# Staging the expert weights of a routed feed-forward layer in eight quarters instead of four

## The chip, the cores and the metric

The kernel runs on one core of one Trainium2 chip. The metric is the device time of one execution in microseconds (us). The engines named below are TensorE (PE in the trace, its weight loads PEld), VectorE (DVE), ScalarE (ACT), GpSimd (POOL) and the queue of SyncE (SP), which issues most transfers.

## What is computed

Three layers follow each other. A recurrent attention gives 3072 tokens of 384 numbers. A dense feed-forward layer (384 to 2048 and back, with W_in and W_out) is applied to them. Then each token goes to the one of 8 experts with the largest gate value, and that expert's two matrices are applied:

```python
e_idx = np.argmax(logits, axis=1)
for e in range(E):
    mask = e_idx == e
    h = np.maximum(x[mask] @ w1[e], 0.0)          # 384 -> 1024
    out[mask] = gate_w[mask, None] * (h @ w2[e])  # 1024 -> 384
```

Results are single precision. Every operand of a large matmul is therefore kept as a sum of two half-precision parts, high and low, and each product is three matmuls: high by high, high by low, low by high.

## The kernel before

**The expert layer in blocks.** Tokens are sorted by expert into blocks of 256. The blocks 0, 1 and 2 (`NB` = 3) are chosen from the first 20 of 24 token tiles, while the dense layer still runs. The experts of the blocks from 3 on are known only when all tokens are routed: `final` writes them as the table `evi2`, and `final_b` the list of tokens in each block. In this run there are 14 blocks, 0 to 13; the last two hold at most 128 tokens each and stand behind branches (`rest`, L1162).

**One block.** `moe_gather` fetches the 256 rows (indirect DMA from POOL) into `G`, `moe_xm` transposes them by DMA into `XM` and copies the gate weights to `GC`. `moe_h(j, m)` computes one eighth (m = 0 to 7) of the hidden layer: nine matmuls into a PSUM bank (`psf` of two banks, or `psa` for m = 2 and 5), ACT's `mt` (ReLU, L881), ACT's `gg` (the high part, L882), and DVE's `gg` (the low part, L336, from `mt` and the high part). `mt` has two buffers: the third `mt` waits for the first's low part. `moe_o(j, t)` multiplies by the second matrix into `pso`, 24 matmuls for each half t of the tokens; the third matmul of every three needs the low part of `gg`. The result is scaled into `ob` and scattered to the output by POOL (L906).

**The weights of a block** come in four quarters q of 768 KB: two of the first matrix (q = 0, 1) and two of the second (q = 2, 3). `moe_w(j, q, e, 0)` loads a quarter into the staging area `SG[q]` from SP's queue (L851 and L853). `moe_w(j, q, None, 1)` converts it into high and low parts: two pieces, each one ACT instruction (L866) and one DVE instruction behind it (L867). The converted matrices are double buffered by parity of the block: W10 and W20 (in the trace `W`) hold even blocks, W11 and W21 odd ones. `SG[0]` and `SG[1]` are tiles of their own, `SG[2]` and `SG[3]` lie in the area `wi` of W_in, each part of which is free once the dense layer has read it for the last time. `conv_q(j, q)` converts quarter q of block j and then loads quarter q of block j + 1 into the same place.

**Block 1 in the program.** `moe_block(1)` runs when the second table appears (`fin`, L957): most of its `moe_o`, `final_b`, the rest of `moe_o`, the first hidden eighths of block 2, the gathers of blocks 3 and 4, and then `conv_q(2, q)` for all four q, which loads block 3.

**What sets the order.** The framework lists each engine's instructions at compile time by a planner that plays the program through with assumed costs. At run time each engine and each queue keeps that order and only waits for semaphores.

Of the kernel before, what the change touches and what calls it, by code (L numbers as in the profile page):

```python
# [10 lines left out]
F32 = mybir.dt.float32  # L11
# [21 lines left out]
MINB = NT // TB  # L33
MAXB = MINB + E - 1
NB = 3
# [18 lines left out]
SR, SA, SV, SS, SG, SX, SWI, SWO, SX2, SWG, SW1, SH2, SW2 = 8, 11, 12, 11, 14, 10, 5, 13, 13, 10, 13, 14, 13  # L54
# [75 lines left out]
def body(ctx, tc, r, k, v, w, u, rk, ul, w_in, w_out, mod, w_gate, bias, w1, w2, cst, out, dbg=None):  # L130
# [173 lines left out]
    z = 2 if wide else 1  # L304
# [521 lines left out]
    def moe_gather(j):  # L826
        idx = FT["idx"] if j < NB else FT["idx2"]
        g_ = G[j % 3]
        nr = NT if j >= NB else NF * 128
        for t in range(2):  # L830
            nc.gpsimd.indirect_dma_start(  # L831
                out=g_[:, t, :], out_offset=None, in_=scr[0:nr],
                in_offset=bass.IndirectOffsetOnAxis(ap=idx[:, 0, 2 * j + t:2 * j + t + 1], axis=0),
                bounds_check=nr - 1, oob_is_err=False,
            )
# [9 lines left out]
        return nc.sync.value_load(et, min_val=0, max_val=E - 1)  # L845

    def moe_w(j, q, e, part):
        st = SG[q]
        if part == 0:
            if q < 2:  # L850
                nc.sync.dma_start(st, w1[ds(e, 1), q].rearrange("e p x -> p (e x)"))  # L851
            else:
                nc.sync.dma_start(st, w2[ds(e, 1), q - 2].rearrange("e p x -> p (e x)"))  # L853
            return
        if q < 2:
            dst = W1[j % 2][:, :, :, 512 * q:512 * q + 512]
            sv, sc = st.rearrange("p (k f) -> p k f", k=KD), SW1
        else:
            dst = W2[j % 2][:, :, 4 * (q - 2):4 * (q - 2) + 4, :]
            sv, sc = st.rearrange("p (k f) -> p k f", k=4), SW2  # L860
        for z_ in range(2):
            if q < 2:
                o_, i_ = dst[:, :, :, 256 * z_:256 * z_ + 256], sv[:, :, 256 * z_:256 * z_ + 256]
            else:
                o_, i_ = dst[:, :, 2 * z_:2 * z_ + 2, :], sv[:, 2 * z_:2 * z_ + 2, :]
            nc.scalar.activation(o_[:, 0], i_, AF.Copy, scale=_pow2(sc))  # L866
            nc.vector.scalar_tensor_tensor(o_[:, 1], i_, _pow2(sc), o_[:, 0], op0=ALU.mult, op1=ALU.subtract)  # L867
# [50 lines left out]
    def load_q(j, q):  # L918
        if q == 0:
            RG[j] = moe_reg(j)  # L920
        moe_w(j, q, RG[j], 0)

    def conv_q(j, q, load=True):
        if CV.get(j, 0) > q:
            return
        CV[j] = q + 1
        with tc.issue_after(END["ib"]) if j in (NB - 1, NB) else ExitStack():
            moe_w(j, q, None, 1)
        if load:
            load_q(j + 1, q)  # L930

    def moe_block(j, nt=2, hook=None, done=0, ahead=0, conv=False, load=False, x=False):
        n = [0]

        def tick():
            if hook:
                hook(n[0])
            n[0] += 1

        def cv(q):  # L940
            if conv:
                conv_q(j + 1, q, load)

        fin = x and j == NB - 2
        if x and j + 2 <= MINB + 1 and j not in (NB - 2, NB - 1):
            moe_xm(j + 2)
        for m in range(NF2):
            tick()
            if m >= done:
                if m == max(done, 3) and not fin:  # L950
                    cv(0)
                moe_h(j, m, 128 * nt)
            if x and m == 5 and j >= NB - 1 and j + 3 <= MINB + 1:
                moe_gather(j + 3)
            if x and m == 5 and j == NB - 1:
                moe_xm(j + 2)
        if fin:  # L957
            for t in range(nt):
                tick()
                moe_o(j, t, 0, NF2 - 3)  # L960
            final_b()
            with tc.issue_after(PLM[0]):
                for t in range(nt):
                    moe_o(j, t, NF2 - 3, NF2)
                for m in range(ahead):
                    moe_h(j + 1, m)
            moe_gather(NB)
            moe_xm(NB)
            moe_gather(NB + 1)
            for q in range(4):  # L970
                cv(q)
            return
        for m in range(ahead):
            moe_h(j + 1, m)
        for t in range(nt):
            tick()
            cv(1 + t)
            moe_o(j, t, 0, NF2 - 3)
        if nt == 1:
            cv(2)  # L980
        cv(3)
        if x and j == MINB - 1:
            conv_q(j + 2, 0, False)
            conv_q(j + 2, 1, False)
        for t in range(nt):
            tick()
            moe_o(j, t, NF2 - 3, NF2)
# [93 lines left out]
    for n in range(NG * NU + LAG):  # L1081
# [11 lines left out]
        if mp is None and sp[0] == len(steps):  # L1093
# [3 lines left out]
            wif = wi.rearrange("p u a k f -> p (u a k f)")  # L1097
            SG = [mp.tile([128, 1536], F32, name=f"SG{i}") for i in range(2)]
            SG += [wif[:, 3072 * i:3072 * i + 3072].bitcast(F32) for i in range(2)]
            XM = [mp.tile([128, 2 * KD, TB], F16, name=f"XM{i}") for i in range(2)]  # L1100
            XM += [wif[:, 6144:6144 + 2 * KD * TB].rearrange("p (k t) -> p k t", t=TB)]
            G = [mp.tile([128, 2, XR], F32, name=f"G{i}") for i in range(2)]
# [143 lines left out]
```

## Time and profile before

| | us |
|---|---|
| median of 3 runs (lowest, highest) | 744.01 (743.41, 747.09) |
| the profiled execution | 748.82 |
| its span, first to last instruction | 747.1 |
| around the span (748.82 - 747.1) | 1.7 |
| PE busy in the span | 707.1 |
| DVE busy, ACT busy | 507.6, 490.5 |

The dense layer ends near 521 us; from 491 us on expert weights are converted, and from 552 us on blocks 2 to 13 run. The profile is of one execution, and a time in the span is counted from its first instruction.

### The profile page before, as it was taken

How to read it: one execution, taken by the hardware profiler on the slowest of the kernel's cores; microseconds unless marked ns; L12 is line 12 of the kernel's file. 1: busy time of each engine (PE TensorE's matmuls, PEld its weight loads, DVE VectorE, ACT ScalarE, POOL GpSimd, SP SyncE). 2: the span in 40 equal slices, each digit the busy share in tenths (PEclk: the TensorE clock that was granted, in tenths of full speed). 3: DMA queues.
4: the chain of work that ended last, by engine and by line, in shares of the span. 5: the costliest groups of instructions: out<-in, count | busy, mean ns of one | idle time of the engine just before them, and what ended most of it. 6: DMA issues, size and time to landing. Idle time of an engine off the chain costs nothing. (4 is left out here: it accounts for less than half of the span.)

```text
span 747.1 us, 17657 instructions
## 1 busy us (share of the span) xinstructions
PE 707.1 (95%) x6769; PEld 536.1 (72%) x6769; DVE 507.6 (68%) x1077; ACT 490.5 (66%) x955; POOL 425.1 (57%) x414
## 2 busy tenths in 40 slices
PE   4899989999999999999999999998998999999984
PEld 4768867777777777777777777776776777767763
DVE  5999984575746665667566645777785789666761
ACT  3568755667666677766666765477755977657752
POOL 5878888778677778877767660012053566231221
PEclk9999989999999999999999999999999999999998
DMA  9875343444423442354331202189439999899930
GB/s 296 264 229 189 125 112 81 122 102 112 101 76 91 118 105 58 100 124 102 80 79 55 32 13 33 54 254 303 142 90 329 374 343 333 244 246 238 258 122 13
DMA packets 89059, 114.77 MB, mean 154 GB/s; under 512 B 60709, under 2 KB 67018, under 8 KB 88964
## 3 DMA queue, kind: packets, MB, share of 16 engines
q1 hardware_dynamic: 84512, 102.75, 49.3%
q0 software_dynamic: 3456, 10.24, 4.3%
q8 instruction: 57, 0.93, 0.5%
q10 hardware_dynamic: 996, 0.53, 0.3%
q14 instruction: 38, 0.31, 0.2%
HBM read 90.29 MB, written 9.84 MB: 134 GB/s over the span
## 5 line engine op out<-in xcount | busy, mean ns | idle before, releaser
L538 PE MATMUL psf<-xT,wi 128*128 128x256 f16 x1728 | 212.9, 277 | 6.5 <-DVE e L547 4.6
L562 PE MATMUL pso<-wo,ring 128*128 128x384 f16 x1152 | 211.3, 327 | 0.8 <-ACT wo L301 0.4
L538 PEld LDWEIGHTS <-wi 128*128 128x128 f16 x1728 | 167.1, 99 | 35.3 <-issue 6.4
L562 PEld LDWEIGHTS <-ring 128*128 128x128 f16 x1152 | 110.7, 98 | 63.2 <-issue 2.0
L336 POOL TENSOR_TENSOR ring<-e,ring 128x512 f16<-128x512 f32 x80 | 92.5, 1157 | 55.0 <-ACT ring L549 51.9
L547 DVE SCALAR_TENSOR_TENSOR e<-e,psf 128x512 f32<-128x512 f32 x96 | 65.7, 685 | 83.0 <-ACT e L546 79.3
L895 PE MATMUL pso<-W,gg 128*128 128x384 f16 x624 | 111.0, 326 | 2.3 <-DVE gg L336 2.3
L875 PEld LDWEIGHTS <-W 128*128 128x128 f16 x1008 | 93.6, 99 | 22.8 <-issue 4.2
L549 ACT ACTIVATE ring<-e 128x512 f16<-128x512 f32 x96 | 60.1, 626 | 52.5 <-DVE e L547 52.2
L895 PEld LDWEIGHTS <-gg 128*128 128x128 f16 x624 | 60.1, 98 | 38.6 <-DVE gg L336 4.7
L906 POOL DMA_INDIRECT out_dram<-ob,idxb x20 | 36.2, 1808 | 86.3 <-DVE ob L905 45.4
L545 ACT ACTIVATE e<-psf 128x512 f32<-128x512 f32 x96 | 56.6, 590 | 31.9 <-PE psf L538 27.8
L546 ACT ACTIVATE e<-e,nel 128x512 f32<-128x512 f32 x96 | 69.1, 720 | 2.4
L867 DVE SCALAR_TENSOR_TENSOR W<-SG,W 128x768 f16<-128x768 f32 x56 | 52.3, 956 | 25.6 <-ACT W L866 25.3
L875 PE MATMUL psf<-XM,W 128*128 128x256 f16 (+1 forms) x540 | 61.3, 266 | 0.9 <-ACT mt L881 0.9
L866 ACT ACTIVATE W<-SG 128x768 f16<-128x768 f32 x56 | 45.3, 835 | 21.8 <-DMA SG<-in_w_dram 21.5
L867 DVE SCALAR_TENSOR_TENSOR W<-wi,W 128x768 f16<-128x768 f32 x56 | 52.0, 955 | 8.6 <-ACT W L866 7.4
L336 DVE TENSOR_TENSOR gg<-mt,gg 128x256 f16<-128x256 f32 (+1 forms) x112 | 43.5, 404 | 10.3 <-ACT gg L882 8.8
L866 ACT ACTIVATE W<-wi 128x768 f16<-128x768 f32 x56 | 44.8, 835 | 5.0 <-DMA wi<-in_w_dram 2.0
L882 ACT ACTIVATE gg<-mt 128x256 f16<-128x256 f32 (+1 forms) x112 | 42.6, 400 | 1.7
L350 DVE TENSOR_TENSOR_SCAN RK<-lw,bnd 112x520 f32<-112x520 f32 x24 | 34.5, 1439 | 8.0 <-ACT lw L349 4.6
L881 ACT ACTIVATE mt<-psf 128x256 f32<-128x256 f32 (+1 forms) x84 | 29.1, 360 | 15.8 <-PE psf L875 8.3
(268 smaller groups left out, 1142.4 us busy)
## 6 DMA issues: line engine op xcount, KB each, us to landing
SG<-in_w_dram SPq DMA_DIRECT2D x28, 768.0 KB, 7.0
wi<-in_w_dram SPq DMA_DIRECT2D x28, 768.0 KB, 5.5
stg<-in_w_in_dram SPq DMA_DIRECT2D x8, 768.0 KB, 4.9
stg<-in_w_out_dram SPq DMA_DIRECT2D x8, 768.0 KB, 4.3
ld<-in_rk_dram SPq DMA_DIRECT2D x16, 384.0 KB, 3.2
lw<-in_w_dram SPq DMA_DIRECT2D x24, 227.5 KB, 2.9
lr<-in_r_dram SPq DMA_DIRECT2D x24, 224.0 KB, 3.0
lk<-in_k_dram SPq DMA_DIRECT2D x24, 224.0 KB, 3.0
```

What stands on the lines that cost most here:

```text
L336: (nc.gpsimd if pool else nc.vector).tensor_tensor(lo, f, hi, op=ALU.subtract)
L538: mm = nc.tensor.matmul(ph[:, 256 * z_:256 * z_ + 256], lhsT=wi[:, u_, a, kk, 128 * z_:128 * z_ + 128], rhs=xg[:, b_ * KD + kk, :], start= ...
L545: nc.scalar.activation(e, ph, AF.Exp, scale=_pow2(-PH))
L546: nc.scalar.activation(e, e, AF.Identity, scale=_pow2(PH), bias=nel)
L547: LASTV[0] = nc.vector.scalar_tensor_tensor(e, e, 0.0, ph, op0=ALU.min, op1=ALU.max).ins
L549: LASTA[0] = nc.scalar.activation(hl[:, 0], e, AF.Copy).ins
L562: nc.tensor.matmul(po_[g][i][:, 0:DM], lhsT=hl[:, a, z_, 128 * i:128 * i + 128], rhs=wo[:, u_, b_, z_, :], start=(u_ + z_ + n == 0), stop= ...
L866: nc.scalar.activation(o_[:, 0], i_, AF.Copy, scale=_pow2(sc))
L867: nc.vector.scalar_tensor_tensor(o_[:, 1], i_, _pow2(sc), o_[:, 0], op0=ALU.mult, op1=ALU.subtract)
L875: nc.tensor.matmul(ph[:, 0:n_], lhsT=w_[:, a, kk, 128 * m:128 * m + 128], rhs=xm[:, b_ * KD + kk, 0:n_], start=(n == 0), stop=(n == 3 * KD ...
L882: nc.scalar.activation(h2[:, 0, m, 0:n_], t_, AF.Copy)
L895: MK[0] = nc.tensor.matmul(po[:, 0:DM], lhsT=h2[:, a, m, 128 * t:128 * t + 128], rhs=w_[:, b_, m, :], start=(m == 0 and a + b_ == 0), stop ...
```

## The change

There are eight staging places instead of four. The new four lie in the area `wo` of W_out, which the dense layer's last matmul (L562, at 521 us) leaves free. Blocks 3, 5, 7, 9, 11 and 13 stage in the new places, all others in the old ones. Converting quarter q of block j now loads block j + 2 (for j = 2 and above) and no longer j + 1; the loads of block 3 get a place of their own in `moe_block(1)`, in front of the conversions of block 2, and can go out as soon as `evi2` is there. The number of loads, conversions and matmuls is the same.

```diff
--- before.py
+++ after.py
@@ -845,7 +845,7 @@
     def moe_w(j, q, e, part):
-        st = SG[q]
+        st = SG[q + (4 if j >= NB and (j - NB) % 2 == 0 else 0)]
         if part == 0:
...
@@ -926,8 +926,9 @@
         CV[j] = q + 1
         with tc.issue_after(END["ib"]) if j in (NB - 1, NB) else ExitStack():
             moe_w(j, q, None, 1)
-        if load:
-            load_q(j + 1, q)
+        nx = j + (1 if j < NB - 1 else 2)
+        if load and nx <= MINB + 1:
+            load_q(nx, q)
...
@@ -967,6 +968,8 @@
             moe_gather(NB)
             moe_xm(NB)
             moe_gather(NB + 1)
+            for q in range(4):
+                load_q(NB, q)
             for q in range(4):
                 cv(q)
             return
@@ -1097,6 +1100,8 @@
             SG = [mp.tile([128, 1536], F32, name=f"SG{i}") for i in range(2)]
             SG += [wif[:, 3072 * i:3072 * i + 3072].bitcast(F32) for i in range(2)]
+            wof = wo.rearrange("p u a z d -> p (u a z d)")
+            SG += [wof[:, 3072 * i:3072 * i + 3072].bitcast(F32) for i in range(4)]
```

The planner sets out the instructions anew from this point on; up to it the orders of all engines are equal. Three places follow.

DVE, right behind the list of tokens (L732), before. The names with 8271, 8285 are the first two hidden eighths of block 2; W10, W20 are block 2's converted weights, W11, W21 block 3's:

```order
L867 SCALAR_TENSOR_TENSOR W20_6977<-wi_71,W20_6977 128x768 x4
L841 COPY GC3_6982<-G0_6973 128x2
L336 TENSOR_TENSOR gg_74<-mt_8271,gg_74 128x256
L867 SCALAR_TENSOR_TENSOR W10_6975<-SG0_6969,W10_6975 128x3x256 x2
L841 COPY GC0_6979<-G1_6974 128x2
L336 TENSOR_TENSOR gg_74<-mt_8285,gg_74 128x256
```

and now:

```order
L867 SCALAR_TENSOR_TENSOR W20_6977<-wi_71,W20_6977 128x768 x4
L867 SCALAR_TENSOR_TENSOR W11_6976<-wo_72,W11_6976 128x3x256 x4
L867 SCALAR_TENSOR_TENSOR W21_6978<-wo_72,W21_6978 128x768 x4
L841 COPY GC3_6982<-G0_6973 128x2
L841 COPY GC0_6979<-G1_6974 128x2
L867 SCALAR_TENSOR_TENSOR W10_6975<-SG0_6969,W10_6975 128x3x256
L336 TENSOR_TENSOR gg_74<-mt_8271,gg_74 128x256
L867 SCALAR_TENSOR_TENSOR W10_6975<-SG0_6969,W10_6975 128x3x256
L336 TENSOR_TENSOR gg_74<-mt_8285,gg_74 128x256
```

The eight low-part conversions of block 3, which stood behind the hidden eighths of block 2, now stand in front of the first low part `gg`.

ACT, a little later, before (8299, 8371 and 8385 are hidden eighths of block 2, 8371 being the one with m = 3; `W11<-SG0` is block 3):

```order
L882 ACTIVATE gg_74<-mt_8285 128x256 [waits Activation_49]
L881 ACTIVATE mt_8299<-psa_8289 128x256 [waits DVE_49,PE_49]
L882 ACTIVATE gg_74<-mt_8299 128x256 [waits Activation_49]
L881 ACTIVATE mt_8371<-psf_8361 128x256 [waits DVE_49,PE_49]
L881 ACTIVATE mt_8385<-psf_8375 128x256 [waits DVE_49]
L882 ACTIVATE gg_74<-mt_8371 128x256 [waits Activation_49]
L882 ACTIVATE gg_74<-mt_8385 128x256 [waits Activation_49]
L881 ACTIVATE mt_8399<-psa_8389 128x256 [waits DVE_49]
L882 ACTIVATE gg_74<-mt_8399 128x256 [waits Activation_49]
L866 ACTIVATE W11_6976<-SG0_6969 128x3x256 [waits DMAHW4_49]
```

and now, where 8384 is the one with m = 3 and `W10<-SG0` with the DMA wait is quarter 0 of block 4:

```order
L882 ACTIVATE gg_74<-mt_8285 128x256 [waits Activation_49]
L881 ACTIVATE mt_8299<-psa_8289 128x256 [waits DVE_49,PE_49]
L882 ACTIVATE gg_74<-mt_8299 128x256 [waits Activation_49]
L866 ACTIVATE W10_6975<-SG0_6969 128x3x256 [waits DMAHW0_49]
L866 ACTIVATE W10_6975<-SG0_6969 128x3x256 [waits DVE_49,PE_49]
L881 ACTIVATE mt_8384<-psf_8374 128x256 [waits DVE_49,PE_49]
L881 ACTIVATE mt_8398<-psf_8388 128x256 [waits DVE_49]
```

The conversion of a quarter that is loaded for block 4 has come in front of the hidden eighth m = 3 of block 2. The semaphore DMAHW0 is that of SP's load `SG0`, which is issued when DVE's second `W10<-SG0` of the list above is done.

SP, before, behind the gathered rows of blocks 3 and 4 (`SG0`, `SG1` are block 3's quarters):

```order
L840 DMA_TRANSPOSE XM0_6971<-G0_6973 128x6x128 x2
L840 DMA_TRANSPOSE XM1_6972<-G1_6974 128x6x128 x2
L851 ISA
L851 DMA SG0_6969<-in_w1_dram 128x1536
L851 ISA
L851 DMA SG1_6970<-in_w1_dram 128x1536
```

and now, right behind the first value that SP reads from `evi2` (`wo` is block 3); twelve more reads and the rows `XM0`, `XM1` follow, and then `SG0` with block 4:

```order
L845 TENSOR_LOAD evi2_7937
L845 ISA x2
L851 ISA
L851 DMA wo_72<-in_w1_dram 128x1536
L851 ISA
L851 DMA wo_72<-in_w1_dram 128x1536
L853 ISA
L853 DMA wo_72<-in_w2_dram 128x1536
L853 ISA
L853 DMA wo_72<-in_w2_dram 128x1536
```

Block 3's loads have moved from behind the transposes to in front of the twelve reads.

## Rows read from the trace of the kernel before

**Rows 1.** The page, busy time of the engines over the span (share, instructions).
```profile
PE 707.1 (95%) x6769; PEld 536.1 (72%) x6769; DVE 507.6 (68%) x1077; ACT 490.5 (66%) x955; POOL 425.1 (57%) x414
```

**Rows 2.** Busy time by stretch: start:end, length, PE, PEld, DVE, ACT, POOL, PEclk, DMA.
```profile
585.00:718.00 133.00, 130.10 (x985) 95.83 (x983) 98.45 (x164) 98.75 (x207) 53.33 (x27) 1.00 0.95 281
540.00:550.00 10.00, 10.00 (x80) 6.85 (x78) 7.69 (x29) 5.99 (x12) 2.02 (x2) 1.00 0.08 29
565.00:570.00 5.00, 2.35 (x14) 1.18 (x14) 1.37 (x3) 2.31 (x5) 2.76 (x3) 0.99 1.03 406
570.00:575.00 5.00, 5.00 (x30) 3.78 (x31) 3.57 (x6) 3.29 (x7) 0.00 (x0) 0.67 1.00 395
105.00:110.00 5.00, 5.00 (x24) 3.03 (x23) 3.25 (x5) 3.02 (x7) 4.76 (x7) 0.59 0.62 213
```

**Rows 3.** Timeline of PE: start, length, line, operation, count, [idle before <- releaser].
```profile
555.32 2.13 PE L875 MATMUL psa<-wi,W 128*128 128x256 f16 x18
557.29 0.81 PE L895 MATMUL pso<-W,gg 128*128 128x384 f16 x4
557.94 1.36 PE L875 MATMUL psf<-wi,W 128*128 128x256 f16 x11
559.14 1.14 PE L895 MATMUL pso<-W,gg 128*128 128x384 f16 x6
560.11 0.93 PE L875 MATMUL psf<-wi,W 128*128 128x256 f16 x7
...
564.14 3.21 PE L895 MATMUL pso<-W,gg 128*128 128x384 f16 x18
570.00 0.61 PE L875 MATMUL psa<-XM,W 128*128 128x256 f16 x2 [2.65 <-ACT W L866]
```

**Rows 4.** Timeline of PE, 585 to 690 us: three of the pauses.
```profile
648.46 1.31 PE L895 MATMUL pso<-W,gg 128*128 128x384 f16 x7 [0.29 <-DVE gg L336]
...
662.45 2.12 PE L875 MATMUL psf<-wi,W 128*128 128x256 f16 x18 [1.22 <-ACT mt L881]
...
678.84 2.13 PE L875 MATMUL psf<-XM,W 128*128 128x256 f16 x18 [0.57 <-ACT mt L881]
```

**Rows 5.** SP's reads of the experts' numbers: ns min/median/max, first and last start.
```profile
L845 SPq TENSOR_LOAD <-evi x14: 260/268/527, 485.7 to 550.7; - x14
...
L845 SPq EVENT_SEMAPHORE  x5: 28/28/11640, 531.3 to 543.2; - x5
```

**Rows 6.** Timeline of DVE behind the list of tokens.
```profile
552.03 1.82 DVE L867 SCALAR_TENSOR_TENSOR W<-SG,W 128x768 f16<-128x768 f32 x2
553.77 3.56 DVE L867 SCALAR_TENSOR_TENSOR W<-wi,W 128x768 f16<-128x768 f32 x4
557.24 0.17 DVE L841 COPY GC<-G 128x2 f32<-128x2 f32 x1
557.31 0.42 DVE L336 TENSOR_TENSOR gg<-mt,gg 128x256 f16<-128x256 f32 x1
557.65 1.85 DVE L867 SCALAR_TENSOR_TENSOR W<-SG,W 128x768 f16<-128x768 f32 x2
```

**Rows 7.** Timeline of ACT in the same stretch.
```profile
552.10 0.58 ACT L903 ACTIVATE ob<-pso,GC 128x384 f32<-128x384 f32 x1 [5.33 <-PE pso L895]
...
554.54 0.38 ACT L881 ACTIVATE mt<-psf 128x256 f32<-128x256 f32 x1 [0.40 <-PE psf L875]
...
568.37 1.58 ACT L866 ACTIVATE W<-SG 128x768 f16<-128x768 f32 x2 [2.66 <-DMA SG<-in_w_dram]
```

**Rows 8.** Timeline of SP's queue: transposes, then block 3's first two loads.
```profile
554.65 6.46 SPq L840 DMA_TRANSPOSE XM<-G  x4
561.38 1.77 SPq L851 DMA_DIRECT2D SG<-in_w_dram  x2
```

**Rows 9.** Landing of L851's loads: those of 480 to 500 us, then all.
```profile
DMA to landing us min/median/max: 4.5/4.9/7.4
...
DMA to landing us min/median/max: 4.5/7.0/8.7
```

**Rows 10.** DVE's waits from 560 us: who waited for whom, total, times, longest.
```profile
DVE ob L905 <- DMA out_dram<-ob,idxb: 7.6, 3, 4.0
```

## Prediction

> **What bounds the kernel now.** I read the page first, then the busy time by stretch, then the timelines of PE, DVE, ACT and SP around the place where the change begins. PE is busy for 95% of the span [rows 1], so a gain must come out of PE's pauses, and only those behind the start of the expert blocks can be touched. There are two kinds. One large pause stands at 567.35 us: PE waits 2.65 us for ACT's conversion of block 3 [rows 3], and ACT waits there for the load of `SG` [rows 7], which went out at 561.38, behind four transposes that held SP's queue from 554.65 [rows 8]. After that pause the granted clock falls: its mean is 0.67 in the five microseconds from 570, where PE works without a break [rows 2]. At half clock (the lower of its two levels, 1.2 GHz) for a part of the time that loses 0.33 x 5 = 1.65 us. The other kind is small: from 585 to 718 us PE is busy 130.1 of 133.0 us [rows 2], 2.9 us of pauses in all. Three of them, 0.29 + 1.22 + 0.57 = 2.08 us, wait for instructions of DVE and ACT that stand behind conversions [rows 4]; most of the rest stands behind `ob`, which waits for scattered output [rows 10]. So the whole that this change could win is 2.65 + 1.65 + 2.9 = 7.2 us.
>
> **What it removes.** Loads, conversions and matmuls keep their number, so no engine gets more to do. Block 3's loads go out when SP has read the first number of `evi2`, at 543.2 us and some tenths [rows 5], and not at 561.38. DMA is nearly idle there (share 0.08) [rows 2]. Even with the longest landing of any such load, 8.7 us [rows 9], the first is there at 553; the four DMA issues delay the twelve further reads by under 0.9 us each (1.77 us for two) [rows 8], so that these end near 554.7 instead of 551.2, just when the transposes could start anyway (554.65) [rows 5, 8]. This part costs nothing, and the load that ACT waits for at 568 is gone.
>
> One price can be weighed against a page. The first loads from this line, up to 500 us, landed in 4.5 to 7.4 us, 4.9 in the median; over the whole span it is 7.0 [rows 9]. The Trainium skill, page "DMA: Bandwidth & Descriptors", section "Anatomy of one DMA — SWDGE (gpsimd) path", fits 2.0 us plus the bytes by 436 GB/s, which makes 3.8 us (an estimate from that page, for another issuing path). By it the sum below would be 1.1 us smaller; I go by the rows.
>
> **What it adds, first wait.** DVE gets through the list of tokens at 552.03 and then does six conversions in 5.21 us, 0.87 each [rows 6]. Before, the first low part `gg` followed at 557.31 and PE used it at 559.14 [rows 3, 6]. Now eight conversions of block 3 stand in between. DVE is in order and their data is long there, so it does them: 557.24 + 8 x 0.87 = 564.2. Then come two copies `GC` (0.07 each), one conversion (0.87), and the low part (0.42) [rows 6]: 565.6. In the meantime PE, from 557.29, has only what needs no low part: four matmuls of `moe_o` (0.65 us), two and nine of `moe_h` (1.20) [rows 3], and nine of block 3's `moe_h` that were moved up, at 1.97/18 = 0.109 each [rows 3], 0.98. That is 2.8 us of work in 8.3 us; PE stands 5.5 us. ACT can't fill it: it runs into the third `mt`, which needs a buffer that this same low part frees.
>
> **What it adds, second wait.** From 565.6 PE has 14 matmuls of `moe_o` at 0.97/6 = 0.162 and 16 of `moe_h` [rows 3], 4.0 us, until 569.6. The next group of `moe_h` needs a PSUM bank that ACT's `mt` of m = 3 empties, and in front of that `mt` now stands the conversion of block 4's first quarter. Its load reuses `SG0`, which DVE frees with the second conversion behind 564.3, at 566.5 by the same prices. A landing of 4.9 us [rows 9] makes 571.4; two conversions on ACT (1.58) and one `mt` (0.38) [rows 7] make 573.4. PE stands 3.8 us. ACT's conversions wait for loads here because the load two blocks ahead and the work of the present block share ACT's one queue.
>
> Behind that the order has nothing that I find late: block 4's other quarters follow their first within the time that ACT needs to come to them, and from block 5 on each load goes out a whole block earlier than before.
>
> **The sum.** PE's pauses from 557.29 to that point: 5.5 + 3.8 = 9.3 us, where there were 2.65: +6.65. The clock fell after a pause of 2.65 us; I take one fall of the same size behind the second wait (1.65 us, as before, so it cancels), and a fall in the 4.0 us of work between the two waits hides in the second. The loads two blocks ahead win the three small pauses, -2.1; those behind `ob` stay. Together +4.5 us: the profiled execution would go from 748.8 to 753.3 and the median from 744.0 to 748.5. (The profiled execution lies 0.6% above the median of the runs shown, and above their highest; I add the same microseconds to the median.)
>
> **Bounds.** The landing of block 4's first load: 4.5 to 8.7 us [rows 9], -0.4 to +3.8 on the sum; I take the median of the first loads and not 7.0, since block 3's loads are done by then and nothing is queued in front of this one. The clock: no fall at all (-1.65) to two that count (+1.65); elsewhere the mean clock was 0.59 over five busy microseconds [rows 2], a loss of 2.05, so a fall needs not be shorter here. The small pauses: 0 to 2.9 won instead of 2.1, +2.1 to -0.8. The likeliest case alone lies between 745.6 and 756.1.
>
> **Rivals.**
>
> *The early load pays (faster).* If the low part reaches PE in time, the pause at 567.35, its clock and the three small pauses go: 744.0 - 2.65 - 1.65 - 2.08 = 737.6 us. The large pause really is a late load [rows 3, 7], which speaks for it; against it stand the eight conversions in front of the first low part, and DVE has no free time to do them in before 557. It decides if the two new waits come to less than 6.4 us. The Trainium skill says the same as a rule ("DMA: Bandwidth & Descriptors", section "Rules for kernel authors": issue the DMA early, compute, wait on its semaphore late); here the wait is not late, as the conversion was moved up with the load. Chance 0.12.
>
> *Only the first wait shows (no change).* If ACT comes to the `mt` of m = 3 by 569.6 without waiting for block 4, the new pause is 5.5 us, +2.85 against before, and with all 2.9 us of the small pauses won the time stays at 744.0. For it: ACT has been idle long enough to take the conversion at once; against it: the load can't go out before DVE frees `SG0`, and the shortest landing [rows 9] still ends at 571.0. Chance 0.24.
>
> *The second wait is long (clearly slower).* Behind block 4's first load seven more go out at once, four of them into the new area. If it lands like a load under traffic, in 8.7 us [rows 9], the second wait is 7.6 us: 748.5 + 3.8 = 752.3. Chance 0.14.
>
> **How the numbers follow.** My forecast has 0.50. About 0.5% (3.7 us) is what a measurement of this kernel can tell from no change: 740.3 to 747.7 us. Of the forecast's own range a seventh lies below 747.7. Slower is 0.43 + 0.14 = 0.57, the same 0.24 + 0.07 = 0.31, faster 0.12. The range from 743.0 to 755.0 leaves out the faster case and the two far ends of the others.
>
> **What the new profile would show.** Right: block 3's loads into `wo` at about 544 us; eight conversions on DVE in a row from 557.2 to 564.2; PE pausing until about 565.6 for DVE's `gg` and again until about 573.4 for ACT, which waits for the load of `SG`; no wait for `SG` or `wo` on ACT from 590 on; PE's pauses from 590 to 720 under 1.5 us. Wrong: a pause of under 6.4 us in all between 557 and 575, or new pauses behind 580, which my reading of the order doesn't show. The most fragile step is the landing of block 4's first load, then the clock behind the pauses.

## The result

| | before | after |
|---|---|---|
| median of all runs so far, us (lowest, highest, runs) | 745.92 (743.41, 749.87, 8) | 753.49 (750.77, 756.90, 8) |
| the profiled execution | 748.82 | 756.9 |
| its span, mean granted clock | 747.1, 0.989 | 755.1, 0.983 |

The changed kernel is slower by 0.8%: the ratio of its runs to those of the kernel before is 1.008, with a 95% interval of 1.0053 to 1.0106. The 8 runs of before hold the three that the prediction was made on; their median of 744.01 was at the fast end.

A part of the difference between the two profiles arises ahead of the place where the programs part. The timeline of VectorE (DVE) in the changed kernel:

```profile
556.61 0.20 DVE L732 TENSOR_TENSOR idxb<-idfb,psa 128x38 int32<-128x38 f32 x1
556.72 1.82 DVE L867 SCALAR_TENSOR_TENSOR W<-SG,W 128x768 f16<-128x768 f32 x2
558.46 3.55 DVE L867 SCALAR_TENSOR_TENSOR W<-wi,W 128x768 f16<-128x768 f32 x4
561.94 7.03 DVE L867 SCALAR_TENSOR_TENSOR W<-wo,W 128x768 f16<-128x768 f32 x8
568.89 0.23 DVE L841 COPY GC<-G 128x2 f32<-128x2 f32 x2
569.03 0.94 DVE L867 SCALAR_TENSOR_TENSOR W<-SG,W 128x768 f16<-128x768 f32 x1
569.90 0.41 DVE L336 TENSOR_TENSOR gg<-mt,gg 128x256 f16<-128x256 f32 x1
...
578.17 1.83 DVE L867 SCALAR_TENSOR_TENSOR W<-SG,W 128x768 f16<-128x768 f32 x2 [6.25 <-ACT W L866]
```

The first conversion behind the list of tokens starts at 556.72 us where it started at 552.03 [rows 6], 4.69 us later, although the program up to there is the same in both. The early falls of TensorE's clock differ from execution to execution: the changed kernel's granted clock was low around 50, 105 and 120 us, the other's around 100. From here on times are therefore counted from the start of L732, the end of the list of tokens. From there to the end the kernel before took 195.2 us (747.1 - 551.9) and the changed one 198.5 (755.1 - 556.6).

Behind that mark DVE does as predicted: eight conversions of block 3 (`W<-wo`) in a row, two copies, one conversion, and the first low part `gg` at 569.90, where 557.31 was its place before [rows 6]. TensorE (PE) in the same stretch, with what it waited for in brackets:

```profile
563.48 0.82 PE L895 MATMUL pso<-W,gg 128*128 128x384 f16 x4 [1.34 <-ACT gg L882]
564.21 1.38 PE L875 MATMUL psf<-wi,W 128*128 128x256 f16 x11
567.33 1.14 PE L875 MATMUL psa<-XM,W 128*128 128x256 f16 x9 [1.75 <-DMA XM<-G]
570.36 2.10 PE L895 MATMUL pso<-W,gg 128*128 128x384 f16 x6 [1.89 <-DVE gg L336]
...
579.19 2.12 PE L875 MATMUL psf<-wi,W 128*128 128x256 f16 x18 [1.75 <-ACT mt L881]
```

The first predicted wait is there in three pieces, 1.34 + 1.75 + 1.89 = 4.98 us, and ends when DVE's `gg` is done. The second is the 1.75 us at 579.19. What ScalarE (ACT) waited for in front of that `mt`, and when the load had gone out:

```profile
577.30 1.58 ACT L866 ACTIVATE W<-SG 128x768 f16<-128x768 f32 x2 [6.06 <-DMA SG<-in_w_dram]
578.78 0.64 ACT L881 ACTIVATE mt<-psf 128x256 f32<-128x256 f32 x2
```

```profile
571.20 1.82 SPq L851 DMA_DIRECT2D SG<-in_w_dram  x2
```

The load of block 4's first quarter went out at 571.20, when DVE had freed `SG0`, and ACT stood 6.06 us in front of it with the `mt` queued behind. The busy time by stretch, columns as in [rows 2]:

```profile
585.00:718.00 133.00, 132.02 (x1007) 98.02 (x1005) 98.15 (x166) 100.09 (x209) 37.60 (x29) 1.00 0.92 279
565.00:570.00 5.00, 1.73 (x15) 1.09 (x12) 5.00 (x9) 0.00 (x0) 2.82 (x2) 0.95 1.04 218
570.00:575.00 5.00, 4.64 (x19) 2.87 (x20) 1.92 (x5) 0.80 (x2) 2.89 (x3) 0.50 0.54 164
575.00:580.00 5.00, 3.25 (x21) 2.07 (x19) 1.83 (x3) 2.70 (x6) 2.46 (x3) 0.87 0.98 357
```

The clock is at half (0.50) for all of 570 to 575, the work between the two waits. From 585 to 718 PE is idle for 0.98 us where it was for 2.9 [rows 2]. The pair closes: 6.73 - 2.65 = +4.1 of pauses in the first 40 us, +1.3 of clock, -1.9 of later pauses, together +3.5, where 3.3 were measured. (The clock's part counts only time in which PE worked; the table behind the experiments has it.) Yet the medians differ by 7.6, and the experiments had to find the rest.

### The profile page after: what moved, and what is told of

Its sections match the earlier page's. It is cut to its first block, busy times and chain, and to the rows that moved or that the text cites. A ratio compares the mean times of both kernels' runs of the same rounds, so it can differ in the third digit from the quotient of the medians.

```text
span 755.1 us, 17660 instructions
## 1 busy us (share of the span) xinstructions
PE 713.0 (94%) x6769; PEld 538.4 (71%) x6769; DVE 514.1 (68%) x1077; ACT 493.3 (65%) x955; POOL 407.9 (54%) x414
## 5 line engine op out<-in xcount | busy, mean ns | idle before, releaser
L562 PE MATMUL pso<-wo,ring 128*128 128x384 f16 x1152 | 212.3, 328 | 3.4 <-DVE X L571 2.2
L562 PEld LDWEIGHTS <-ring 128*128 128x128 f16 x1152 | 110.5, 98 | 67.0 <-issue 5.5
L895 PE MATMUL pso<-W,gg 128*128 128x384 f16 x624 | 112.7, 329 | 6.0 <-DVE gg L336 4.6
L906 POOL DMA_INDIRECT out_dram<-ob,idxb x20 | 27.3, 1363 | 88.6 <-DVE ob L905 50.4
L867 DVE SCALAR_TENSOR_TENSOR W<-wo,W 128x768 f16<-128x768 f32 x48 | 44.9, 955 | 5.5 <-ACT W L866 4.3
L350 DVE TENSOR_TENSOR_SCAN RK<-lw,bnd 112x520 f32<-112x520 f32 x24 | 38.1, 1589 | 9.6 <-ACT pso L364 5.0
L866 ACT ACTIVATE W<-wo 128x768 f16<-128x768 f32 x48 | 39.5, 838 | 7.1 <-DMA wo<-in_w_dram 3.3
L867 DVE SCALAR_TENSOR_TENSOR W<-SG,W 128x768 f16<-128x768 f32 x32 | 30.1, 953 | 15.7 <-ACT W L866 13.4
L906 POOL DMA_INDIRECT out_dram<-ob,idxa x6 | 6.9, 1152 | 57.5 <-ACT ob L903 34.1
```

Of the source, the lines that this page charges most:

```text
L562: nc.tensor.matmul(po_[g][i][:, 0:DM], lhsT=hl[:, a, z_, 128 * i:128 * i + 128], rhs=wo[:, u_, b_, z_, :], start=(u_ + z_ + n == 0), stop= ...
L895: MK[0] = nc.tensor.matmul(po[:, 0:DM], lhsT=h2[:, a, m, 128 * t:128 * t + 128], rhs=w_[:, b_, m, :], start=(m == 0 and a + b_ == 0), stop ...
```

## The experiments

Three theories stood at the start. Theory 1 is the prediction's: two waits that the order makes, so that mending the order gives the time back. Theory 2: the loads two blocks ahead cost by their traffic on the DMA engines, so that a mended order leaves the ratio at 1.005 to 1.010. Theory 3: most of the loss is falls of the clock ahead of L732 that differ by chance between executions. Every ratio below is to runs of the kernel before on the same chip; PE's pauses are quoted from PE's timeline.

**again**: the changed kernel once more, no edit.

> The changed kernel itself once more, for a second profile and more rounds. Theory 1: ratio 1.005 to 1.011; counted from L732, the first wait 4.5 to 5.5 us and the second 1.7 to 4 us, where L732 itself falls 550 to 553 us behind the start if the 4.7 us that it came late in the first profile were chance, and at 556 to 557 if the change causes them. Theory 3 (mostly chance upstream): ratio under 1.005 in these rounds.

Measured: 754.58 us, ratio 1.0108 (1.0071 to 1.0146).

```profile
561.52 0.82 PE L895 MATMUL pso<-W,gg 128*128 128x384 f16 x4 [1.18 <-ACT gg L882]
564.14 1.14 PE L875 MATMUL psa<-XM,W 128*128 128x256 f16 x9 [0.52 <-DMA XM<-G]
568.56 1.15 PE L895 MATMUL pso<-W,gg 128*128 128x384 f16 x6 [3.28 <-DVE gg L336]
576.24 3.52 PE L875 MATMUL psf<-wi,W 128*128 128x256 f16 x18 [3.48 <-ACT mt L881]
```

The pieces are others but the first wait is again 1.18 + 0.52 + 3.28 = 4.98 us: DVE's chain sets it. The second is 3.48 us where the work between ran at full clock. L732 fell at 554.8, between the two answers that the expectation allowed. The ratio is Theory 1's and not Theory 3's (under 1.005).

**low_first**, **block4_late**, **both**: the conversions of block 3 on DVE, of block 4 on ACT, or both, are queued behind work of block 2. `LO` and `HI` remember the low part (DVE) and the high part (ACT) of each hidden eighth.

```diff
-        lowp(h2[:, 1, m, 0:n_], t_, h2[:, 0, m, 0:n_], PSM)
+        LO[j, m] = nc.vector.tensor_tensor(h2[:, 1, m, 0:n_], t_, h2[:, 0, m, 0:n_], op=ALU.subtract).ins
...
-        with tc.issue_after(END["ib"]) if j in (NB - 1, NB) else ExitStack():
+        with tc.issue_after(LO[NB - 1, 2]) if j == NB else tc.issue_after(END["ib"]) if j == NB - 1 else tc.issue_after(HI[NB - 1, NF2 - 1]) if j == NB + 1 else ExitStack():
             moe_w(j, q, None, 1)
```

This is both. Low_first lacks the branch for `NB + 1`; block4_late lacks that for `NB`, which keeps `END["ib"]`.

> The change stays whole, but DVE takes block 3's eight conversions behind the low part of block 2's m = 2 and not in front of the one of m = 0. Theory 1 (the time went into two waits that the order makes: DVE's conversions in front of the first low part, ACT's conversion of block 4 in front of an mt): the first wait (4.98 us) goes, and the second as well, since DVE now frees SG0 some 7 us earlier, so that block 4's first load is there before ACT comes to it. Against the kernel before: -2.65 for its large pause, -1.9 for the small ones, 0 to -1.7 for the clock fall behind the large pause: 739.5 to 743 us against 745.9, a ratio of 0.992 to 0.997. Theory 2 (loads two blocks ahead load the DMA queues and slow gathers, transposes and scattered output): the loads are the same, so the ratio stays at 1.005 to 1.010. Theory 3 (the slower time is mostly clock falls upstream that differ from run to run): the ratio would be 1.000 to 1.005 here as in any kernel of this family.

Measured: 752.87 us (750.76 without its two longest runs), ratio 1.0067 (1.0033 to 1.0100).

```profile
557.99 0.82 PE L895 MATMUL pso<-W,gg 128*128 128x384 f16 x4 [1.27 <-ACT gg L882]
562.25 0.50 PE L895 MATMUL pso<-W,gg 128*128 128x384 f16 x2 [2.15 <-DVE gg L883]
571.17 1.47 PE L895 MATMUL pso<-W,gg 128*128 128x384 f16 x8 [1.13 <-DVE gg L883]
574.10 0.38 PE L875 MATMUL psa<-XM,W 128*128 128x256 f16 x2 [1.45 <-ACT mt L881]
```

The eight conversions are out of the way of the first low part, and still PE stands 6.00 us, in four other places. At 562.25 it is DVE's copy of `GC` out of a gathered `G`, in front of the low part in the queue; at 557.99 ACT's eight conversions, which come to an end at the pace of the loads. At 571.17 it is the moved piece itself, which DVE does in front of the next low parts:

```profile
563.75 7.03 DVE L867 SCALAR_TENSOR_TENSOR W<-wo,W 128x768 f16<-128x768 f32 x8
```

At 574.10 it is ACT's conversion of block 4 again, which waits 1.47 us for its load. The ratio alone would fit Theory 2. Theory 1 was right on what made the two waits and wrong on what removing them is worth.

> The change stays whole, but ACT takes block 4's conversions only behind the last hidden eighth of block 2, so that no mt of that block stands behind one of them; block 3's eight conversions stay in front of the first low part. Theory 1: the first wait stays (about 5.0 us between the line L732 and 18 us behind it), the second (1.75 us, 3.8 without the half clock in front of it) goes. Against the kernel before: +5.0 - 2.65 - 1.9 and 0 to +1.7 for the longer fall of the clock: 746.4 to 748.1 us against 745.9, a ratio of 1.001 to 1.003. If the first wait is the whole loss, the ratio stays at 1.006 or above. Theory 2 (DMA load): 1.005 to 1.010. Theory 3 (chance upstream): 1.000 to 1.005.

Measured: 760.06 us, ratio 1.0192 (1.0153 to 1.0232), far above the ranges of all theories (1.010 at most; only "1.006 or above" was left open upward). The second wait is gone, the first one is 4.25 us (1.16 + 2.85 + 0.24). A pause of another kind stands behind, on PE and on DVE:

```profile
656.99 2.42 PE L895 MATMUL pso<-W,gg 128*128 128x384 f16 x7 [6.87 <-DVE gg L883]
```

```profile
655.99 0.62 DVE L905 TENSOR_SCALAR ob<-pso,GC 128x384 f32<-128x384 f32 x1 [8.45 <-DMA out_dram<-ob,idxb]
```

DVE waits 8.45 us for scattered output to leave `ob`, and the low parts are queued behind.

> Both edits in one: block 3's conversions on DVE behind the third low part of block 2, block 4's on ACT behind block 2's last hidden eighth. Theory 1: no pause of over 1 us of TensorE between L732 and 30 us behind it, a ratio to the kernel before of 0.992 to 0.997, within 1 us of the run that only moves DVE's conversions, as that one frees SG0 early too. If block 4's conversion costs something apart from its load, this one is faster than the other by over 2 us. Theory 2 (DMA load): 1.005 to 1.010. Theory 3 (chance upstream): 1.000 to 1.005.

Measured: 751.00 us, ratio 1.0060 (1.0031 to 1.0090). PE's pauses of over 1 us are not gone: 2.84 us for ACT's `gg` at 559.89, 1.16 and 1.34 us at 581 and 583. The ratio is again in Theory 2's range and not in Theory 1's (0.992 to 0.997).

From here the theories were others. Theory A: the early loads cost by themselves. Theories B and C: loading two blocks ahead costs.

**early_only** keeps the early loads and loads one block ahead from there on; **two_ahead_only** loads block 3 at the place in the program where the kernel before did, but into the new area, and goes two blocks ahead from block 4. It is not free of early loads: as the new area is free early, block 3's first quarter goes out at 545.39 us, ahead of the transposes, where the kernel before had all four behind them [rows 8].

```diff
 # early_only
-        st = SG[q + (4 if j >= NB and (j - NB) % 2 == 0 else 0)]
+        st = SG[q + (4 if j == NB else 0)]
...
-        nx = j + (1 if j < NB - 1 else 2)
-        if load and nx <= MINB + 1:
+        nx = j + 1
+        if load and nx != NB:
 # two_ahead_only
-            for q in range(4):
-                load_q(NB, q)
...
+        if load and j == NB - 1:
+            load_q(NB, q)
```

> Early loads of block 3 as in the change, with the same eight conversions in front of the first low part and block 4's in front of an mt, but one block ahead from there on as before the change. Theory A: both waits stay as they are (5.0 to 5.5 and 1.75 to 3.5 us), the small pauses come back (about 2 us): ratio 1.009 to 1.014. Theory C (loads two ahead are the cost, by the traffic behind 580): under 1.004.

Measured: 751.89 us, ratio 1.0066 (1.0037 to 1.0096).

```profile
560.30 0.82 PE L895 MATMUL pso<-W,gg 128*128 128x384 f16 x4 [1.19 <-ACT gg L882]
563.00 1.14 PE L875 MATMUL psa<-XM,W 128*128 128x256 f16 x9 [0.59 <-DMA XM<-G]
567.34 2.10 PE L895 MATMUL pso<-W,gg 128*128 128x384 f16 x6 [3.20 <-DVE gg L336]
...
576.51 2.13 PE L875 MATMUL psf<-wi,W 128*128 128x256 f16 x18 [2.52 <-ACT mt L881]
```

Both waits are as in the whole change, the first 4.98 us for the third time. The small pauses did not come back: between 577 and the tail PE pauses nowhere. So the ratio is under what Theory A gave (1.009 to 1.014), and over what Theory C did (under 1.004). Theory 2 can't be the whole cause either: this version loads one block ahead and is slower by 0.7% all the same.

> Block 3's quarters are loaded where the kernel before had them (only the first of them goes out ahead of the transposes), into the new area, and from block 4 on loads run two blocks ahead as in the change. Theory A: no wait in front of the first low part beyond two conversions (under 1 us of TensorE), the large pause of 2.65 us stays or grows to at most 5 us since block 4's loads now go out beside block 3's, the small pauses go: ratio 0.997 to 1.004. Theory C: 1.008 or above.

Measured: 751.26 us, ratio 1.0057 (1.0032 to 1.0081).

```profile
561.98 0.38 PE L875 MATMUL psa<-XM,W 128*128 128x256 f16 x2 [2.52 <-DMA XM<-G]
...
669.19 0.60 PE L895 MATMUL pso<-W,gg 128*128 128x384 f16 x2 [3.39 <-DVE ob L905]
```

The large pause for weights is gone, and 2.52 us for block 3's tokens stand in its place: as the weights of the first quarter are there early, the order moves two matmuls of block 3 (`psa<-XM`) in front of ready work of block 2, and the transposed tokens are not there. The ratio lies between Theory A's range (up to 1.004) and Theory C's (from 1.008). Each of the two versions costs 4 to 5 us of median, by different waits.

**half_early** and **conv_behind** go after Theory A. The first loads only two quarters early, with DVE's conversions of them behind the third low part; the second keeps the four loads and queues ACT's conversions too behind block 2's third eighth.

```diff
 # half_early, beside LO[NB - 1, 2] for j == NB and q < 2
-            for q in range(4):
+            for q in range(2):
                 load_q(NB, q)
...
+        if load and j == NB - 1 and q >= 2:
+            load_q(NB, q)
 # conv_behind, beside LO[NB - 1, 2] for j == NB
+            tc.issue_after(HI[NB - 1, 2]) if j == NB else ExitStack()
```

> Two ahead as in the change, but only block 3's first two quarters are loaded early; its last two go out behind the four transposes. DVE's conversions of the first two stand behind the third low part of block 2, the others follow where the planner puts them. Theory A (the early loads cost by themselves: four of them share the DMA engines, the last lands 11 us after the first was issued, ACT's eight conversions end late in front of the first mt, and the gathers behind them land 2 to 3.5 us later): half the bytes are through before the gathers go out, so ACT reaches the first mt where it did before, DVE waits under 1 us for a gathered G, TensorE's pauses from L732 to 30 us behind it are under 1.5 us in all, and the ratio to the kernel before is 0.992 to 0.999. Theory B (what is left in the last runs is not from the early loads but from loading two ahead): 1.004 to 1.010, as with both edits.

Measured: 753.67 us, ratio 1.0099 (1.0065 to 1.0133). ACT is in time, as Theory A said, but PE waits 3.39 us for `XM` at 564.62, the same wait as in two_ahead_only, and 4.14 us for DVE's `ob` at 671.60. The ratio is the one that Theory B gave.

> All four early loads stay, but ACT's eight conversions of block 3 too stand behind block 2's third hidden eighth. This tells the two ways apart in which the early loads could cost. If it is ACT's queue (conversions waiting for loads in front of the first mt), TensorE's pauses in the 12 us behind L732 go to under 0.5 us and the ratio falls to 0.995 to 1.002. If it is the DMA engines (gathers and transposes behind 3.1 MB of weights), a pause for XM or GC of 1.5 to 3.5 us stays and the ratio is 1.003 to 1.008.

Measured: 757.60 us, ratio 1.0149 (1.0102 to 1.0196). Neither answer came. No pause is for `XM` or a gather, and the loss is larger:

```profile
560.52 0.94 PE L875 MATMUL psf<-wi,W 128*128 128x256 f16 x7 [1.31 <-DVE W L867]
564.16 1.80 PE L875 MATMUL psa<-XM,W 128*128 128x256 f16 x14 [0.96 <-DVE W L867]
568.93 0.82 PE L895 MATMUL pso<-W,gg 128*128 128x384 f16 x4 [1.01 <-ACT gg L882]
571.44 2.51 PE L895 MATMUL pso<-W,gg 128*128 128x384 f16 x8 [1.68 <-DVE gg L883]
...
654.64 2.42 PE L895 MATMUL pso<-W,gg 128*128 128x384 f16 x7 [4.14 <-DVE gg L883]
```

Eight conversions are 7.03 us of DVE and 8 x 0.79 = 6.3 us of ACT. In one piece they hold up whatever stands behind, wherever the piece is put. In the kernel before, the landing of the loads spaces them (in the next profile two at 569.46 us, a low part at 571.20, two at 573.18, each pair behind an ACT that waits for the load).

**before_again**: the kernel before, profiled a second time.

> The kernel before, profiled once more. The medians of the runs differ by 6 to 8 us where the two profiles differ by 3.3 from L732 on. If the large pause of 2.65 us and the clock fall behind it belong to the kernel, L732 falls 550 to 557 us behind the start and the rest takes 194.5 to 196 us again (195.2 in the first profile). If the first profile of it was an unlucky one, the pause is shorter or the fall missing, and the rest takes 190 to 193 us; the change then had less to win than the first profile showed.

Measured: 745.48 us, one run; L732 at 551.9, and 191.8 us from there to the end (743.7 - 551.9). PE's timeline has these pauses behind L732 and no other, the last two in the tail:

```profile
561.64 1.47 PE L895 MATMUL pso<-W,gg 128*128 128x384 f16 x8 [0.58 <-DVE GC L841]
570.21 0.43 PE L875 MATMUL psa<-XM,W 128*128 128x256 f16 x2 [2.21 <-ACT W L866]
717.50 0.83 PE L875 MATMUL psa<-XM,W 128*128 128x128 f16 x12 [0.89 <-issue]
721.06 0.82 PE L895 MATMUL pso<-W,gg 128*128 128x384 f16 x4 [1.40 <-DVE gg L336]
```

The large pause belongs to the kernel (2.21 us), and so does the fall of the clock behind it. The 2.9 us of small pauses do not: they belonged to the first execution, and so did most of ACT's waits for loads in that stretch. From 590 to 718 us ACT waited for loads of `SG`, in before and then in before_again (total, times, longest):

```profile
ACT W L866 <- DMA SG<-in_w_dram: 13.4, 4, 4.3
```

```profile
ACT W L866 <- DMA SG<-in_w_dram: 2.5, 3, 1.1
```

In an execution like the second the change had less to win than [rows 4] showed. Which of the two is the more usual, two profiles can't tell; the second is nearer to the median of the runs (745.48 against 745.92).

**two_half_xm** and **one_half_xm**: half_early with TensorE's matmuls of block 3 queued behind block 2's last eighth, two blocks ahead and one block ahead. In the second, block 3's last two quarters are loaded behind the transposes of its tokens and converted on ACT behind block 2's sixth eighth.

```diff
+                with tc.issue_after(MH[0]) if j == NB and n == 0 else ExitStack():
                     mm = nc.tensor.matmul(
...
+                if j < NB:
+                    MH[0] = mm
```

> As half_early, but TensorE takes block 3's first matmuls only behind the last hidden eighth of block 2, not as soon as the weights are there. Theory D (the wait for weights was replaced by one for block 3's tokens: the order moves block 3's matmuls up as their weights come early, and TensorE then stands in front of a transposed gather with ready work queued behind): the pause of 3.39 us for XM goes without another of over 1 us between L732 and 25 us behind it, and with it a clock fall: 4 to 5 us less than half_early, 748 to 750 us, a ratio to the kernel before of 1.001 to 1.005 (the waits for scattered output behind 660 stay). If the pause only moves on to another wait: ratio 1.008 to 1.012 as for half_early.

Measured: 756.16 us, ratio 1.0112 (1.0077 to 1.0147). The pause for block 3's `XM` is gone and others stand near it (0.92, 1.68, 0.77, 0.49 us, three of them for ACT's `mt`), and behind 660 again 1.23 and 4.19 us for DVE's `ob`. The second answer, "only moves on", is what came.

> The same with one block ahead from block 4 on: block 3's first two quarters early, its last two behind the transposes of its tokens, DVE's conversions behind the third low part, TensorE's matmuls of block 3 behind block 2's. Theory D and that loads two ahead cost waits for scattered output: no pause of over 1 us from L732 to the tail, 744 to 747 us, a ratio of 0.994 to 1.002. If early loads cost in any form: 1.004 or above.

Measured: 751.02 us, ratio 1.0062 (1.0034 to 1.0090). No wait for scattered output reaches PE, but two others do: 2.15 us at 565.91, behind a `GC` copy that waits for a gather, and 4.71 us at 581.89 for ACT, which waits for block 4's first load.

```profile
580.26 1.58 ACT L868 ACTIVATE W<-SG 128x768 f16<-128x768 f32 x2 [5.64 <-DMA SG<-in_w_dram]
```

The ratio is that of the answer "if early loads cost in any form".

**all_edits**: the whole change with every such place mended at once.

```diff
+        with tc.issue_after(LO[NB - 1, 2]) if j in (NB, NB + 1) else ExitStack():
             nc.vector.tensor_copy(GC[j % 4], g_[:, :, DM:XR])
...
+        with tc.issue_after(LO[NB - 1, 2]) if j == NB else tc.issue_after(END["ib"]) if j == NB - 1 else tc.issue_after(HI[NB - 1, min(5 + q, 7)]) if j == NB + 1 else ExitStack(), (
+            tc.issue_after(HI[NB - 1, 4]) if j == NB and q >= 2 else ExitStack()
+        ):
             moe_w(j, q, None, 1)
```

TensorE's matmuls of block 3 are queued as in two_half_xm.

> Early loads and two blocks ahead as in the change, and the order mended at every place that the runs so far showed: DVE takes block 3's conversions, and the copies GC that wait for gathers, behind the third low part of block 2; ACT takes only block 3's first two quarters early and the last two behind block 2's fifth eighth, and block 4's behind its sixth to eighth; TensorE takes block 3's matmuls behind block 2's last eighth. If the loss is made of waits that the order puts in front of ready work, no pause of over 1 us is left between L732 and 30 us behind it, L732 to the end takes 188 to 191 us (191.8 in the second profile of the kernel before), and the ratio is 0.994 to 1.000. If the DMA engines, busy from there on, set the pace whatever the order is, a wait for a load, a gather or scattered output takes the place again and the ratio is 1.004 to 1.010.

Measured: 753.49 us, ratio 1.0125 (1.0072 to 1.0178), the six runs from 745.97 to 761.80, with a median of 751.22 without the two longest. The profiled execution was the fastest of them: 193.2 us from L732 to the end, and its pauses in the first 40 us are many and small (0.58, 0.15, 1.56, 1.31, 0.46, 1.12), 5.18 us together. So the first answer is refuted: two pauses are over 1 us within 30 us, and the rest took more than 191 us. Of the second answer a part came: the 1.56 us are for ACT, which waited 2.31 us for block 4's load. No version beat the kernel before.

**All profiles in one sum.** For each profile: the time from L732 to the end; PE's pauses in the first 40 us and from there to 160 us behind L732; the clock's loss (for each microsecond behind L732, PE's busy time times the part of full speed that was not granted, summed); and what is left when these and the tail's pauses (2.3 us in each) are taken off. Only busy time counts, as the clock also falls behind the last matmul, which ends some 10 us before the span does, and costs nothing there. In before_again, columns as in [rows 2]:

```profile
736.00:741.00 5.00, 0.00 (x0) 0.00 (x0) 0.00 (x0) 0.00 (x0) 0.00 (x0) 0.67 0.04 7
```

| profile | L732 to end | pauses, first 40 us | pauses, 40 to 160 us | clock | left |
|---|---|---|---|---|---|
| before | 195.2 | 2.65 | 2.89 | 1.7 | 185.7 |
| before_again | 191.8 | 2.79 | 0.00 | 1.6 | 185.1 |
| after | 198.5 | 6.73 | 0.98 | 3.0 | 185.5 |
| again | 199.2 | 8.46 | 0.89 | 1.7 | 185.9 |
| early_only | 197.4 | 7.50 | 0.00 | 2.5 | 185.1 |
| two_ahead_only | 196.7 | 2.52 | 4.37 | 1.7 | 185.8 |
| half_early | 199.9 | 3.39 | 4.33 | 4.6 | 185.3 |
| conv_behind | 203.3 | 5.16 | 5.62 | 4.6 | 185.6 |
| two_half_xm | 199.7 | 4.16 | 5.73 | 1.7 | 185.8 |
| one_half_xm | 198.2 | 7.15 | 1.67 | 1.6 | 185.5 |
| low_first | 195.1 | 6.00 | 1.28 | 0.0 | 185.5 |
| both | 195.5 | 5.34 | 0.00 | 3.0 | 184.9 |
| block4_late | 203.5 | 4.79 | 6.87 | 4.2 | 185.3 |
| all_edits | 193.2 | 5.18 | 0.31 | 0.0 | 185.4 |

What is left is 184.9 to 185.9 us in all of them. Behind L732 nothing but PE's pauses and the clock tells these kernels apart.

## Why the prediction was right, point by point

**Direction and size.** Forecast 748.5 us with 743.0 to 755.0, on a base of 744.0; measured 753.5, and 745.9 to 746.4 for the base. Slower by over 0.5% was the likeliest case and is what came. The size is in part luck: the forecast difference was +4.5 us, the medians differ by 7.6, and the time lies near the upper end of the range. The pauses of the first 40 us grew by less than forecast (by 4.1 us in the pair, not 6.65), while the small pauses were not won and some microseconds came ahead of L732, of which the prediction says nothing.

**First wait.** Predicted 13.7 us from L732 to the first low part's end, 565.6 - 551.9; measured 569.90 + 0.41 - 556.61 = 13.7. The pause is 4.98 us and not 5.5, as PE had 3.3 us of work and not 2.8. This step is shown: of the four profiles with the eight conversions in front three have 4.98 us each and one 4.25, and with them elsewhere (low_first, both) they are no longer what PE waits for there.

**Second wait.** Predicted 3.8 us; 1.75 in the first profile, where PE did the work ahead of it at half clock and so came late to the wait, and 3.48 and 2.52 in the profiles of again and early_only. The mechanism is shown by ACT's row of 6.06 us in front of the load and by block4_late, where the wait is gone. Landing was 6.1 us at most in the first profile, from 571.20 to 577.30; in again it was 4.9 at most (569.40 to 574.34), as forecast, and in early_only 6.4 (568.18 to 574.61).

**The clock.** I let it cancel. Behind L732 it cost 1.7 and 1.6 us in the two profiles of before, 3.0 in the first of the changed kernel and 1.7 in the second: once it cancelled, once it added 1.3.

**The small pauses**, -2.1 us: this term failed. Against the profile that the prediction was made on, the pauses went from 2.9 to 0.98 us, and the sign "no wait for `SG` or `wo` on ACT from 590 on" is there in both profiles of the changed kernel. But the second profile of the kernel before has none, so against that execution the change wins nothing there and adds 0.9 to 1.0. With 0 in place of -2.1 the sum is +6.65, and the two profiles of the changed kernel lie 6.7 and 7.4 us above that second one from L732 on. That these agree is chance in part: the sum leaves out the added 0.9 to 1.0 and the clock, and puts the pauses of the first 40 us 0.8 to 2.6 us too high (9.3 against 8.46 and 6.73). One of the three pauses was also misread: the 0.29 us at 648.46 stand behind an `ob` that had waited 3.96 us for scattered output, not only behind conversions.

**"This part costs nothing"**, said of the early loads: only the delay of SP's reads was weighed. The four loads share the DMA engines. Alone, one of them landed in 4.9 us, four together in 7.6 in the median:

```profile
wo<-in_w_dram SPq DMA_DIRECT2D x1, 768.0 KB, 4.9
```

```profile
wo<-in_w_dram SPq DMA_DIRECT2D x4, 768.0 KB, 7.6
```

The first row is of two_ahead_only from 540 to 560 us, the second of again from 540 to 565. ACT's conversions, in order, came to an end at the pace of the loads, and PE lost 1.34 us to that at 563.48. It did not add to the sum, as DVE's chain ended later, but it is the next wait in low_first and both (1.27 and 2.84 us). The busy time by stretch has the DMA engines busy for 0.90 of the time there, against 0.21 before; the first row is of after, the second of before_again:

```profile
550.00:560.00 10.00, 10.00 (x88) 6.90 (x86) 7.15 (x19) 6.35 (x11) 3.76 (x4) 1.00 0.90 359
```

```profile
545.00:555.00 10.00, 10.00 (x87) 6.80 (x86) 7.16 (x19) 2.96 (x8) 3.94 (x4) 1.00 0.21 66
```

359 GB/s at a busy share of 0.90 are 399 when busy. The Trainium skill, page "DMA: Bandwidth & Descriptors", section "Where 436 GB/s comes from", gives 435 as the ceiling of the ports that the 16 engines share, and about 358 as the limit that binds for transfers from the chip's main memory (HBM). The row with 359 lies under the first, as does the estimate of 399 when busy, which lies over the second.

**The rivals.** That the early load pays is refuted twice: early_only, the early loads alone, has a ratio of 1.0066. Its point of decision, new waits under 6.4 us, was passed with 6.73 and 8.46. The Trainium skill's rule beside it (page "DMA: Bandwidth & Descriptors", section "Rules for kernel authors": issue early, wait late) did not pay here either: the weights came early, and conversions and matmuls were pulled up in front of older work with them. That only the first wait shows is refuted by the second wait in three profiles. That the second wait is long (7.6 us) did not come either: it was 3.48 us at most.

**What stays open.** Behind L732 the two profiles of after lie 5.4 us in the mean above the two of before; the medians of the runs lie 7.6 and 8.2 apart. The mean clock of the runs (0.986 against 0.991 in the median) is worth 3.7 us over 745, of which the profiles show 0.7 behind L732. So some 2 to 3 us seem to lie ahead of L732, where the programs are the same. L732 fell at 551.9 in both profiles of before, and between 550.5 and 557.6 (mean 553.5) in the twelve others, and it goes with the early falls of the clock: they cost 1.7 us in the four profiles with L732 at 551.0 to 551.9, and 6.8 in the four with 554.1 to 557.6. In the two profiles of before they cost 3.4 and 1.7 us, in the two of the changed kernel 6.8 and 5.1. Why the changed kernel has more of them, by chance or by something like the code's placing, was not tried. DVE waits longer for scattered output in the changed kernel, as DVE's waits show from 560 us on (who waited for whom, total, times, longest), after first and again behind:

```profile
DVE ob L905 <- DMA out_dram<-ob,idxb: 11.3, 3, 6.9
```

```profile
DVE ob L905 <- DMA out_dram<-ob,idxb: 13.9, 4, 7.2
```

Before it was 7.6 us [rows 10], in before_again and early_only nothing, in one_half_xm 3.5: 0 to 7.6 us in the four profiles that load one block ahead, and 4.1 to 13.9 in the ten that load two. The ranges overlap, so loading two blocks ahead makes it more likely and does not decide it. In five of the eight edited versions that load two blocks ahead such a wait cost PE 3 to 7 us in one place, in the others under 1.3. Why the output leaves later was not tested; that it shares the DMA engines with the loads is only argued, and they were as busy in the kernel before (share 1.08 and 1.07 from 560 to 580 us in its two profiles).

## What to carry to other kernels

Data that comes early also pulls its consumers forward: where a planner orders by readiness, early weights put their conversions and matmuls in front of older work on queues that are in order, so move the load and pin the consumers, and count where each engine would find time for the whole piece. A late load can also be what spaces long work out. Before a pause is counted as a gain, profile the kernel before a second time: of 7.2 us that looked winnable here, 2.9 were not there in the next execution.

## What the runs showed of the hardware that was not expected

- The clock does not fall behind each pause. It fell behind 2.21 and 2.65 us (before_again, before), 2.84 (both) and 3.39 (half_early), but not behind 2.52 us in two_ahead_only, nor in low_first, whose four pauses of 1.13 to 2.15 us make 6.00, nor in all_edits (six, 5.18 us together).
- Early in the run, falls of the clock come and go between executions of the same instructions: they cost from 1.7 to 6.8 us ahead of L732 in the fourteen profiles.
- Scattered output can take so long to leave that an engine waits 8.45 us for its buffer (block4_late), where the longest such wait before was 4.0 [rows 10].
